# Local and global attention feeding a squared-ReLU MLP: heads loaded ahead of the transpose in SP's queue, value products on 128 columns of weights, and the second global pair's jobs a slot or two later

## The chip, the core and the metric

The kernel runs on one core of one Trainium2 chip. The metric is the device time of one execution in microseconds. Of the kernel before there are three timed runs, 1212.3, 1215.22 and 1217.07 us, median 1215.22 us. One more execution was profiled.

## The reference, cut to what matters

The input has 8 batches of 8 heads. Each head has 512 local positions and 32 global ones, all with 64 features. A local position attends to the local keys at most 32 positions away and to all 32 global keys; a global position attends to every key. The 64 features of the 8 heads are then put side by side, and a two-layer MLP with a squared ReLU follows.

```python
s_g = scale * np.matmul(q_g, k_all.transpose(0, 1, 3, 2))
out_g = np.matmul(sm(s_g), v_all)
...
s_l = np.concatenate([s_lg, s_ll], axis=-1)
a_l = sm(s_l)
out_l = np.matmul(a_l, np.concatenate([v_g, v_l], axis=2))
...
h = np.maximum(x @ w_in, 0.0)
return (h * h @ w_out).astype(np.float32)
```

## The kernel before, in words

**Work items.** A work item is one head of one batch on one half (256 queries) of the local positions. There are 128 such items, numbered `t`; the text calls them heads. Eight heads that share a batch and a half form a group of 256 tokens, which is one block of the MLP. The 16 groups give 16 blocks, and the global tokens of all batches (8 x 32) form a 17th. Each block takes 8 MLP steps, numbered `m`.

**The slot.** The main loop (L590) has one iteration per head, called a slot here. Slot `t` carries the attention of head `t`, the end of the attention of head `t - 1`, and MLP step `m = t - 9`. For the heads from 16 on ("not plain") the stations of a head are these:

- `load_head` (L91) loads queries and keys into `raw` (128 x 608 fp32), `load_v` (L103) loads the values into `v`. Both go through SP's queue. Both tiles have two buffers, so head `t + 2` can only be loaded into the buffer that head `t` has left.
- `split_qk` (L133) rounds `raw` to fp32r on ACT, and `split_qk_rest` (L143) makes the low parts on DVE. It runs in the slot before the one that uses it: slot `t` splits head `t + 1`.
- `scores` (L150, tile `s`) on PE, `softmax1` on DVE, `softmax2` (the exponentials) on ACT, `softmax3` (sums, reciprocal, scaling) on DVE; the result is `prob`, which has one buffer.
- `turn` (L218) splits the fp32 words of `prob` into two planes of 16 bits with three POOL copies into `planes`, and SP issues a DMA transpose of `planes` into `turned`. One slot later `join` (L226) puts the halves together again on POOL, into `joined`.
- `av` (L231) multiplies values and `joined` on PE in fp32, into the PSUM tile `xa`: three products of 256, 128 and 128 moving columns, each of them two instructions on PE. `x_evac` splits `xa` into `x_h` (ACT) and `x_l` (DVE), which the MLP reads nine slots later.

The plain heads (0 to 15) load query, key and value in one transfer and transpose on PE instead; their value products (tile names `pts` and `raw` in the rows) already take 128 columns of weights.

**PE in a slot.** `scores(t)` (rows `s`, four instructions), `gemm1` (rows `h`, 24), the global scores (rows `gs`, one), the first half of `gemm2` (rows `o`, six), `av(t - 1)` (rows `xa`, six), and the second half of `gemm2` (`o`, six). All but `xa` are fp32r.

**Global jobs.** Twice in 16 slots a set of four heads' global attention is carried through as a chain of jobs (L660 to L679), hung on slots relative to a slot `d`: maximum, exponential, `g_turn` and `g_join` (the same trip through POOL and the DMA transpose), `g_parts`, and for each of two pairs of heads a load of values, `g_split_v` (one ACT cast, two DVE subtractions), `g_av` (13 matmuls, rows `gxo`, and one ACT copy) and `g_x` (four DVE transposes). The number behind a job's slot is its place in the slot: 6 and 3 lie behind `turn`, 0 lies between `gemm1` and `gemm2`, 1 at the end of the slot. The two sets of 16 slots have `d` = 27 and 32, then 43 and 48, and so on, so that the tail of one lies beside the head of the next.

**What sets the order.** Every engine runs its instructions in the order of its queue. From slot 17 on, calls through the wrappers `pe`, `ve`, `ac`, `po`, `sp` are kept in the order in which the program makes them (L592); calls on `nc.sync` directly (`qr`, `gv`, the output) are put where the scheduler sees room. In slot `t` SP's calls were: `load_v(t)`, the transpose of `turn(t)`, `load_head(t + 2)`.

Of the kernel before, what the change touches and what calls it, by code (L numbers as in the profile page):

```python
# [7 lines left out]
F32 = mybir.dt.float32  # L8
# [9 lines left out]
P = 128  # L18
HALF = 256
NGR = 2 * B  # L20
NT = NGR * H
QC, KC, VC = HALF, 352, 256
QK, PK = QC + KC, QC + KC + VC
PS = QK + 192
WIN = 224
NEG = -1.6e10
NBLK = NGR + 1
# [2 lines left out]
NPLAIN = 16  # L30
# [8 lines left out]
def f(ap):  # L39
    return ap.bitcast(F32)  # L40
# [19 lines left out]
def attention_moe(  # L60
# [10 lines left out]
    pe, ve, ac, po, sp = (InOrder(tc, e) for e in (nc.tensor, nc.vector, nc.scalar, nc.gpsimd, nc.sync))  # L71
# [3 lines left out]
    p2 = ctx.enter_context(tc.tile_pool(name="p2", bufs=2))  # L75
# [3 lines left out]
    ps_a = ctx.enter_context(tc.tile_pool(name="ps_a", bufs=1, space=PSUM))  # L79

    heads = {}

    def plain(t):
        return t < NPLAIN
# [3 lines left out]
    def w_take(n):  # L88
        w_bufs["free"] -= n

    def load_head(t):  # L91
        if plain(t):
            w_take(1)
            raw = wp.tile([P, 1024], F32, tag="w", name=f"raw{t}")[:, :PK]
        else:
            raw = p2.tile([P, QK], F32, tag="raw", name=f"raw{t}")
        if t == 0:
            nc.sync.dma_start(raw[:, : QC + KC], pk[t, :, : QC + KC])
        else:
            sp.dma_start(raw, pk[t, :, : raw.shape[1]])  # L100
        heads[t] = dict(raw=raw)

    def load_v(t):  # L103
        v = heads[t]["v"] = p2.tile([P, 192], F32, tag="v", name=f"v{t}")
        sp.dma_start(v, pk[t, :, QK:PS])

    load_head(0)
    con = cp.tile([P, P + 4 * WIN], F32, name="con")
# [24 lines left out]
    def split_qk(t):  # L133

        if plain(t):
            return
        hd = heads[t]
        raw = hd["raw"]
        hi = hd["hi"] = p2.tile([P, QK + QC], F32R, tag="qk", name=f"qk{t}")
        hd["lo"] = hi[:, QK:]  # L140
        ac.copy(hi[:, :QK], raw[:, :QK])
# [66 lines left out]
    def transposes(t):  # L208
        pr = heads[t]["pr"]
        for i, (o, n) in enumerate(((0, 128), (320, 128), (128, 96), (224, 96))):  # L210
            pe.transpose(pt[:n, 128 * i : 128 * i + 128], pr[:, o : o + n], ident)

    def pt_copy(t):
        pts = p2.tile([P, 512], F32, tag="gh", name=f"pts{t}")
        ac.copy(pts, pt)
        heads[t]["pts"] = pts
# [9 lines left out]
    def join(t):  # L226
        joined = heads[t]["pts"] = p2.tile([P, 512], F32, tag="joined", name=f"joined{t}")
        words = joined.bitcast(U16).rearrange("p (n h) -> p h n", h=2)
        po.tensor_copy(words, turned.rearrange("p (h c) n -> p h (c n)", h=2))

    def av(t):  # L231
        hd = heads[t]
        c = QC + KC
        if plain(t):

            xa = ps_a.tile([P, HALF], F32, tag="xa", name=f"xa{t}")
            v, pts = hd["raw"][:, c:], hd["pts"]
            mm = [
                (xa, v[:, 0:128], pts[:, 256:512]),
                (xa[:, 0:128], v[:, 64:192], pts[:, 0:128]),  # L240
                (xa[:, 128:256], v[:, 128:256], pts[:, 128:256]),
            ]
        else:
            xa = ps_a.tile([64, HALF], F32, tag="xa", name=f"xa{t}")
            v, pts = hd["v"], hd["pts"]
            mm = [
                (xa, v[:, 128:], pts[:, 128:384]),
                (xa[:, 0:128], v[:, 0:64], pts[:, 0:128]),
                (xa[:, 128:256], v[:, 64:128], pts[:, 384:512]),
            ]  # L250
        for i, (o, a, b) in enumerate(mm):
            pe.matmul(o, a, b, start=i == 0, stop=i == len(mm) - 1, skip_group_check=True)
        hd["xa"] = xa[:64, :]
# [304 lines left out]
    def w_tick(t, place):  # L558
        if t < len(PLAN):
            for c in PLAN[t].split(",")[place]:  # L560
                {"b": w_pass, "s": w_chunk}[c]()

    def w_need(m):

        if m < 8:
            while w_next["bits"] < 8 * m + 8:
                n = w_next["bits"]
                w_pass()
                assert w_next["bits"] > n
        elif m < 16:  # L570
            while not set(range(4 * (m - 8), 4 * (m - 8) + 4)) <= whi.keys():
                n = w_next["split"]
                w_chunk()
                assert w_next["split"] > n, (m, w_next, w_bufs, sorted(w_used)[-1:])
# [15 lines left out]
    for t in range(NSTEP + LAG + 1):  # L590
        m = t - LAG
        ve.on, ac.on, pe.on, po.on, sp.on = [t >= x for x in FREE]  # L592
        prev, run = 1 <= t <= NT, 0 <= m < NSTEP
        live, early = t < NT, t < NPLAIN
        if t < NPLAIN - 8:
            load_head(t + 8)
        if run:
            w_need(m)
        old = prev and plain(t - 1)
        new = prev and not old  # L600
        if old:
            transposes(t - 1)
        if new:
            join(t - 1)
        if live and not early:
            load_v(t)
            scores(t)
        if old:
            pt_copy(t - 1)
        done = 0 < m <= NSTEP and m % 8 == 1 and m > 8  # L610
        if done:
            evac(m // 8 - 1)
        if live:
            softmax1(t)
        if run:
            gemm1(m, 0)
        if t + 1 < NT and not early and not done:
            split_qk(t + 1)
        if live:
            softmax2(t)  # L620
        if t + 1 < NT and not early and done:
            split_qk(t + 1)
        if live and not early:
            softmax3(t)
            turn(t)
        for job, *args in jobs.pop((t, 6), ()):
            job(*args)
        if NPLAIN <= t + 2 < NT:
            load_head(t + 2)
        for job, *args in jobs.pop((t, 3), ()):  # L630
            job(*args)
        w_tick(t, 0)
        if live and early:
            g_scores(t)
        if run:
            gemm1(m, 1)
        if old:
            av(t - 1)
        if live and not early:
            g_scores(t)  # L640
        if early and t + 1 < NPLAIN:
            scores(t + 1)
        if run:
            act1(m)
        if old:
            x_evac(t - 1)
            w_take(-1)
        if early:
            softmax3(t)
        w_tick(t, 1)  # L650
        if t + 1 == NPLAIN:
            split_qk(t + 1)
        if t + 1 < NT:
            split_qk_rest(t + 1)
        if live:
            if t % 2 == 1:
                g_evac(t)
            if t % 4 == 3 and t + 1 < NT:
                g_load(t + 1)
        if live and t % 4 == 3 and (t // 8) % 2 == 1:  # L660
            d = t if t % 8 == 3 else t + 1
            for at, *job in (
                (d + 1, 3, g_soft),
                (d + 1, 1, g_exp),
                (d + 2, 3, g_norm),
                (d + 2, 1, g_load_v, 0),
                (d + 3, 6, g_turn),
                (d + 4, 6, g_join),
                (d + 4, 3, g_split_v, 0),
                (d + 4, 1, g_load_v, 1),  # L670
                (d + 5, 3, g_parts),
                (d + 6, 0, g_av, 0),
                (d + 6, 1, g_split_v, 1),
                (d + 6, 1, g_x, 0),
                (d + 7, 0, g_av, 1),
                (d + 7, 1, g_x, 1),
            ):
                place, job, *args = job
                jobs.setdefault((at, place), []).append((job, t, *args))  # L679
        for job, *args in jobs.pop((t, 0), ()):  # L680
            job(*args)
        if m == NSTEP:
            for i in range(2):
                gemm2(m - 1, 0, (i,))
                gemm2(m - 1, 1, (i,))
                evac(NBLK - 1, (i,))
        elif m > 0:
            gemm2(m - 1, 0)
        if new:
            av(t - 1)  # L690
        if 0 < m < NSTEP:
            gemm2(m - 1, 1)
        if run:
            act2(m)
        if new:
            x_evac(t - 1)
        w_tick(t, 2)
        for job, *args in jobs.pop((t, 1), ()):
            job(*args)
        if 0 < m <= 8:  # L700
            w_done(m - 1)
        w_tick(t, 3)
        if 8 * NGR - 2 <= m < 8 * NGR:
            cols = (slice(0, 224), slice(224, HALF))[m % 2]
            ac.copy(x_h[:, 0, :, cols], xg[:, :, cols])
            ve.tensor_sub(x_l[:, 0, :, cols], xg[:, :, cols], f(x_h[:, 0, :, cols]))
# [75 lines left out]
```

## Time and profile before

The profiled execution took 1213.34 us on its own clock; its span from the first to the last instruction is 1211.6 us, so 1.7 us lie around it. It is 1.9 us under the median of the three timed runs.

| what | value |
|---|---|
| timed runs | 1212.3, 1215.22, 1217.07 us; median 1215.22 us |
| profiled execution, time / span | 1213.34 us / 1211.6 us |
| mean granted PE clock | 0.975 |
| DVE busy, share of the span | 645.9 us, 53% |
| ACT busy, share of the span | 618.3 us, 51% |
| POOL busy, share of the span | 400.4 us, 33% |

In the rows of the profile, PE is the matmul engine, PEld its weight loads, DVE the vector engine, ACT the scalar engine, POOL GpSimd and SPq the queue of SyncE, which issues the DMAs. A row of a timeline gives start and duration in us, then engine, line, operation, the tile written and the tiles read, and, in brackets, how long the engine had been idle and what ended that. L53 is the line of the wrapper, so the tiles tell the operations apart. A row of the chain of waits gives start, duration and the link.

### The profile page before, as it was taken

The page shows a single profiled execution, that of the slowest core. Times are in us where ns is not written, and L with a number is a line of the kernel's source. Part 1 is how long each engine was busy: PE and PEld are TensorE (multiplying, and loading weights), DVE is VectorE, ACT ScalarE, POOL GpSimd, SP SyncE. Part 2 cuts the span into 40 slices and gives each one's busy share as a digit, 9 for nine tenths or more (in the row PEclk, how much of TensorE's full clock was granted, in tenths as well). Part 3 has the DMA queues.
Part 4 walks back from the last instruction along what each step waited for, and adds up shares of the span by engine and source line. Part 5 has one row for each costly group of instructions (what it writes and reads, how often), then busy time and mean ns, then how long its engine had stood idle before and what let it go on. Part 6 is the DMA issues. An engine that isn't in the chain of part 4 may idle for free.

```text
span 1211.6 us, 19435 instructions
## 1 busy us (share of the span) xinstructions
PE 1101.4 (91%) x6704; PEld 913.3 (75%) x6704; DVE 645.9 (53%) x1997; ACT 618.3 (51%) x1519; POOL 400.4 (33%) x543
## 2 busy tenths in 40 slices
PE   8999899888998989979899889988999898999998
PEld 6776787777877768767776677777777676778987
DVE  5698655465554554555554755545454565544210
ACT  6897445464454545454544644545455454545332
POOL 1003433434334343334333443343433443433000
PEclk9999899999998999999999999999999999999999
DMA  9764434434444534345343434434434444343000
GB/s 369 276 222 91 94 93 103 91 102 91 96 105 102 109 90 109 77 99 126 81 106 81 108 93 101 94 91 111 91 81 109 91 116 97 93 90 71 23 18 18
DMA packets 209698, 127.63 MB, mean 105 GB/s; under 512 B 145344, under 2 KB 184768, under 8 KB 209600
## 3 DMA queue, kind: packets, MB, share of 16 engines
q1 hardware_dynamic: 209456, 126.33, 41.8%
q8 instruction: 53, 0.87, 0.3%
q14 instruction: 45, 0.37, 0.1%
q10 hardware_dynamic: 144, 0.07, 0.0%
HBM read 82.84 MB, written 8.91 MB: 76 GB/s over the span
## 4 chain that ended last, share of the span: by engine, by line
DMA 27%; PE 19%; ACT 16%; DVE 13%; POOL 10%; SPq 8%; issue 7%; POOLq 0%; DVEq 0%; ACTq 0%
DMA raw<-in_pk_dram 26%; POOL planes L53 8%; ACT prob L53 8%; SPq L53 8%; PE o L53 8%; PE h L53 7%; ACT qk L53 5%; DVE prob L53 3%; DVE st L53 3%; DVE qk L53 2%; PE xa L53 2%; POOL gp L53 2%; DMA turned<-planes 1%; PE s L53 1%; DVE gl L53 1%
## 5 line engine op out<-in xcount | busy, mean ns | idle before, releaser
L53 PE MATMUL h<-x_h,ws 128*128 128x256 f32 x2048 | 405.3, 291 | 0.0
L53 PEld LDWEIGHTS h<-x_h,ws 128*128 128x128 f32 x2048 | 341.9, 199 | 0.8
L53 PE MATMUL o<-ws,gh 128*128 128x512 f32 x1024 | 336.6, 410 | 0.0
L53 ACT CAST qk<-raw 128x608 fp32r<-128x608 f32 x112 | 78.3, 699 | 445.0 <-DMA raw<-in_pk_dram 444.9
L53 PE MATMUL h<-x_l,ws 128*128 128x256 f32 x1024 | 297.2, 290 | 0.0
L53 POOL COPY planes<-prob 128x448 uint16<-128x448 uint16 x336 | 190.3, 603 | 278.2 <-DVE prob L53 278.2
L53 POOL COPY joined<-turned 128x1024 uint16<-128x1024 uint16 x112 | 151.4, 1352 | 345.1 <-DMA turned<-planes 323.2
L53 DVE TENSOR_SCALAR st<-st 128x2 f32<-128x2 f32 x128 | 23.4, 183 | 381.4 <-ACT prob L53 377.4
L53 PEld LDWEIGHTS o<-ws,gh 128*128 128x128 f32 x1024 | 177.3, 190 | 43.7 <-issue 19.0
L53 PEld LDWEIGHTS h<-x_l,ws 128*128 128x128 f32 x1024 | 204.3, 200 | 1.0 <-DVE x_l L53 0.2
L53 PE MATMUL o<-ws,gl 128*128 128x512 f32 x512 | 203.4, 397 | 0.0
L53 PE MATMUL xa<-joined,v 128*64 128x128 f32 (+1 forms) x672 | 120.7, 316 | 37.5 <-POOL planes L53 24.3
L53 PEld LDWEIGHTS xa<-joined,v 128*64 128x64 f32 x672 | 76.5, 136 | 98.1 <-POOL planes L53 33.1
L53 PE MATMUL s<-qk 128*128 128x224 f32 x448 | 89.6, 306 | 61.5 <-DVE qk L53 56.5
L53 PEld LDWEIGHTS s<-qk 128*128 128x128 f32 x448 | 71.1, 200 | 96.5 <-ACT x_h L53 32.7
L53 DVE TENSOR_TENSOR qk<-raw,qk 64x352 fp32r<-64x352 f32 x224 | 132.4, 591 | 19.5 <-ACT qk L53 13.1
L53 DVE TENSOR_TENSOR gl<-pt,gh 128x512 fp32r<-128x512 f32 x128 | 87.2, 681 | 82.0 <-ACT gh L53 81.9
L53 PEld LDWEIGHTS o<-ws,gl 128*128 128x128 f32 x512 | 97.0, 189 | 22.9
L53 ACT ACTIVATE prob<-prob,st 128x224 f32<-128x224 f32 x224 | 105.8, 473 | 12.1 <-DVE st L53 12.1
L53 ACT ACTIVATE pt<-h 128x512 f32<-128x512 f32 x128 | 73.8, 577 | 66.3 <-PE h L53 66.1
L53 DVE CUSTOM_DVE_ANT_0 prob<-s,con 128x224 f32<-128x224 f32 x224 | 78.0, 385 | 24.0 <-PE s L53 21.4
L53 ACT ACTIVATE pt<-pt 128x512 f32<-128x512 f32 x128 | 74.5, 582 | 4.0
(74 smaller groups left out, 1182.2 us busy)
## 6 DMA issues: line engine op xcount, KB each, us to landing
raw<-in_pk_dram SPq DMA_DIRECT2D x113, 304.0 KB, 3.2
wr<-in_w_dram SPq DMA_DIRECT2D x32, 512.0 KB, 7.4
v<-in_pk_dram SPq DMA_DIRECT2D x112, 96.0 KB, 2.9
gv<-in_vg_dram SPq DMA_DIRECT2D x32, 320.0 KB, 3.8
out_dram<-ot SPq DMA_DIRECT2D x32, 256.0 KB, 3.6
raw<-in_pk_dram SPq DMA_DIRECT2D x15, 432.0 KB, 8.3
qr<-in_qg_dram SPq DMA_DIRECT2D x31, 64.0 KB, 2.8
turned<-planes SPq DMA_TRANSPOSE x112, 3.1
```

Source lines behind the costliest of these rows:

```text
L53: r = method(*args, **kwargs)
```

## The change

The changed kernel issues `load_head(t + 2)` at the start of slot `t`, ahead of `load_v(t)` and of `turn(t)`; before, it came behind `turn(t)`. `load_v` brings 256 instead of 192 columns, and the three value products take 128 columns of weights each, where they took 64, and write all 128 partitions of `xa`; the 64 extra rows of the result are not read. In the global jobs `g_split_v` of the second pair moves from slot `d + 6` to `d + 7` (and to place 3), `g_x` of the first pair from `d + 6` to `d + 8`, `g_av` of the second pair from `d + 7` to `d + 8` and its `g_x` from `d + 7` to `d + 9`; for the last set this last job stays in `d + 8`.

```diff
     def load_v(t):
-        v = heads[t]["v"] = p2.tile([P, 192], F32, tag="v", name=f"v{t}")
-        sp.dma_start(v, pk[t, :, QK:PS])
+        v = heads[t]["v"] = p2.tile([P, VC], F32, tag="v", name=f"v{t}")
+        sp.dma_start(v, pk[t, :, QK:PK])
...
-            xa = ps_a.tile([64, HALF], F32, tag="xa", name=f"xa{t}")
+            xa = ps_a.tile([P, HALF], F32, tag="xa", name=f"xa{t}")
             v, pts = hd["v"], hd["pts"]
             mm = [
                 (xa, v[:, 128:], pts[:, 128:384]),
-                (xa[:, 0:128], v[:, 0:64], pts[:, 0:128]),
-                (xa[:, 128:256], v[:, 64:128], pts[:, 384:512]),
+                (xa[:, 0:128], v[:, 0:128], pts[:, 0:128]),
+                (xa[:, 128:256], v[:, 64:192], pts[:, 384:512]),
             ]
...
         if new:
             join(t - 1)
+        if NPLAIN <= t + 2 < NT:
+            load_head(t + 2)
         if live and not early:
             load_v(t)
             scores(t)
...
-        if NPLAIN <= t + 2 < NT:
-            load_head(t + 2)
...
                 (d + 6, 0, g_av, 0),
-                (d + 6, 1, g_split_v, 1),
-                (d + 6, 1, g_x, 0),
-                (d + 7, 0, g_av, 1),
-                (d + 7, 1, g_x, 1),
+                (d + 7, 3, g_split_v, 1),
+                (d + 8, 3, g_x, 0),
+                (d + 8, 0, g_av, 1),
+                ((d + 8, 1, g_x, 1) if t == NT - 1 else (d + 9, 3, g_x, 1)),
```

The first place is SP's queue around slots 44 and 45. The number in a tile's name is the head (in `qr48` the head whose queries it serves), the rows `turned` are the transposes of `turn(44)` and `turn(45)` before, and of `turn(43)` and `turn(44)` in the changed kernel. Before:

```order
L53 DMA raw45_3471<-in_pk_dram 128x608
L285 DMA qr48_3842<-in_qg_dram 128x128
L53 DMA v44_3522<-in_pk_dram 128x192
L53 DMA_TRANSPOSE turned_95<-planes_94 128x8x128
L53 DMA raw46_3557<-in_pk_dram 128x608
L53 DMA v45_3605<-in_pk_dram 128x192
L53 DMA_TRANSPOSE turned_95<-planes_94 128x8x128
L53 DMA raw47_3640<-in_pk_dram 128x608
```

The same part of SP's queue in the changed kernel:

```order
L52 DMA raw45_3436<-in_pk_dram 128x608
L52 DMA v43_3438<-in_pk_dram 128x256
L52 DMA_TRANSPOSE turned_95<-planes_94 128x8x128
L52 DMA raw46_3522<-in_pk_dram 128x608
L284 DMA qr48_3842<-in_qg_dram 128x128
L52 DMA v44_3524<-in_pk_dram 128x256
L52 DMA_TRANSPOSE turned_95<-planes_94 128x8x128
L52 DMA raw47_3605<-in_pk_dram 128x608
```

The pattern of a transpose followed by a head and a value tile is the same, but the head that follows the transpose of `turn(t)` was `t + 2` and is now `t + 3`: every head stands one transpose earlier.

The second place is DVE's queue at the end of slot 33 and in slot 34, beside the global set of `d` = 27. The rows `ISA` are `softmax1`, the two rows `TENSOR_SCALAR` and `RECIPROCAL` on `st34` with the row on `prob` are `softmax3`, and `STREAM_TRANSPOSE` is `g_x`. Before:

```order
L53 TENSOR_TENSOR x_l_89<-xa32_2577,x_h_88 64x256
L53 TENSOR_TENSOR gvl27_1_2594<-gv27_1_2408,gvh27_1_2593 128x512
L53 TENSOR_TENSOR gvh27_1_2593<-gv27_1_2408,gvh27_1_2593 32x128
L53 STREAM_TRANSPOSE xg_90<-gxs27_0_2569 32x32 x4
L53 ISA prob_93,st34_2618<-s34_2607,con_78 128x224
L53 ISA st34_2618 128x1
L53 ISA prob_93,st34_2618<-s34_2607,con_78 128x224
L53 ISA st34_2618 128x1
L53 TENSOR_SCALAR st34_2618<-st34_2618 128x2
L53 RECIPROCAL st34_2618<-st34_2618 128x2
L53 TENSOR_SCALAR prob_93<-prob_93,st34_2618 128x224 x2
```

The same part of DVE's queue in the changed kernel:

```order
L52 TENSOR_TENSOR x_l_89<-xa32_2577,x_h_88 64x256
L52 ISA prob_93,st34_2611<-s34_2600,con_78 128x224
L52 ISA st34_2611 128x1
L52 ISA prob_93,st34_2611<-s34_2600,con_78 128x224
L52 ISA st34_2611 128x1
L52 TENSOR_SCALAR st34_2611<-st34_2611 128x2
L52 RECIPROCAL st34_2611<-st34_2611 128x2
L52 TENSOR_SCALAR prob_93<-prob_93,st34_2611 128x224 x2
L52 TENSOR_TENSOR gvl27_1_2640<-gv27_1_2408,gvh27_1_2639 128x512
L52 TENSOR_TENSOR gvh27_1_2639<-gv27_1_2408,gvh27_1_2639 32x128
```

The two subtractions of `g_split_v` move from ahead of the softmax of head 34 to behind it, and the four transposes leave this stretch; they now stand in slot 35. The first value product of the pair stays where it was on PE, and the second pair's 13 rows `gxo` move from slot 34 to slot 35. The order on POOL does not change.

More of the change, by code (lines that the diff above doesn't have):

```diff
@@ L23 @@
 QK, PK = QC + KC, QC + KC + VC
-PS = QK + 192
 WIN = 224
```

## The prediction

> **What bounds the kernel now.** I read the page first: busy shares, then the chain that ended last.
>
> ```profile
> PE 1101.4 (91%) x6704; PEld 913.3 (75%) x6704; DVE 645.9 (53%) x1997; ACT 618.3 (51%) x1519; POOL 400.4 (33%) x543
> ...
> DMA raw<-in_pk_dram 26%; POOL planes L53 8%; ACT prob L53 8%; SPq L53 8%; PE o L53 8%; PE h L53 7%; ACT qk L53 5%; DVE prob L53 3%; DVE st L53 3%; DVE qk L53 2%; PE xa L53 2%; POOL gp L53 2%; DMA turned<-planes 1%; PE s L53 1%; DVE gl L53 1%
> ```
>
> PE is busy 91%, so at first sight the matmuls bound it. But the chain passes through PE for 19% of the span only and through the landing of `raw` for 26%: some loop runs through that transfer. The chain in order of time shows it whole, here for one slot:
>
> ```profile
> 602.91 0.70 ACT qk L53
> 603.61 0.95 ACT prob L53 x4
> ...
> 604.99 0.35 DVE prob L53
> ...
> 607.16 1.23 SPq L53
> ...
> 608.45 3.30 DMA raw<-in_pk_dram
> 611.77 0.70 ACT qk L53
> ```
>
> ACT casts one head (602.91), does the exponentials of the head before it, DVE scales, POOL copies the planes, SP issues their transpose (1.23 us), and only behind it in SP's queue the next `raw` (608.45), which lands 3.3 us later; then ACT casts again, 8.86 us after the first cast. ACT runs in order, so everything behind the cast waits too. The row of the list of waits, and two casts from ACT's timeline, give the pace:
>
> ```profile
> ACT qk L53 <- DMA raw<-in_pk_dram: 444.9, 103, 7.2
> ```
>
> ```profile
> 103.79 0.70 ACT L53 CAST qk<-raw 128x608 fp32r<-128x608 f32 x1 [0.84 <-DMA raw<-in_pk_dram]
> ...
> 1090.09 0.70 ACT L53 CAST qk<-raw 128x608 fp32r<-128x608 f32 x1 [4.52 <-DMA raw<-in_pk_dram]
> ```
>
> ACT waits for `raw` 103 times, 444.9 us. The casts are those of heads 18 and 127, the third and the last of 112. From the one to the other are 109 slots and 986.3 us: **9.05 us a slot**, which is the loop's length, longer where a global transpose stands in SP's queue too. Of PE alone a slot needs less. Three stretches, from the table of windows (length, then PE busy, PEld, DVE, ACT, POOL, granted clock, DMA):
>
> ```profile
> 981.24:989.51 8.27, 8.27 (x62) 7.13 (x61) 5.98 (x24) 4.65 (x12) 2.94 (x5) 1.00 0.68 194
> 1061.17:1068.61 7.44, 7.44 (x50) 6.32 (x48) 4.14 (x14) 4.28 (x12) 3.03 (x4) 1.00 0.23 63
> 1130.00:1209.00 79.00, 76.29 (x490) 68.11 (x488) 13.62 (x27) 27.69 (x49) 0.00 (x0) 1.00 0.05 16
> ```
>
> The second is a slot without any PE idle: 7.44 us. The first is one with the 13 `gxo` matmuls, 8.27 us, so these cost 0.83 us. In both DVE, ACT and POOL are busy for 6 us or less. The third, the MLP alone at the end, has PE busy 76.3 of 79 us, and its clock is 1.00. So PE idles some 1.4 us a slot for a loop that PE isn't in.
>
> **The change: loading ahead.** The transfers and their order in the queue keep their pattern, but the head behind a given transpose is one further on. It is issued at the same moment and needed a slot later: 3.3 us of landing against more than 7. The wait of 444.9 us goes. What `load_head(t + 2)` itself waits for is the last read of `raw` of head `t`, by DVE in slot `t - 1`:
>
> ```profile
> 606.82 0.70 PE L53 MATMUL s<-qk 128*128 128x224 f32 x4
> ...
> 607.16 1.23 SPq L53 DMA_TRANSPOSE turned<-planes  x1
> ...
> 607.96 0.39 DVE L53 CUSTOM_DVE_ANT_0 prob<-s,con 128x224 f32<-128x224 f32 x1
> ...
> 608.45 0.57 SPq L53 DMA_DIRECT2D raw<-in_pk_dram  x1
> ...
> 609.12 0.39 SPq L53 DMA_DIRECT2D v<-in_pk_dram  x1
> ...
> 610.34 1.35 POOL L53 COPY joined<-turned 128x1024 uint16<-128x1024 uint16 x1 [3.20 <-DMA turned<-planes]
> ...
> 614.32 1.68 POOL L53 COPY planes<-prob 128x448 uint16<-128x448 uint16 x3 [2.63 <-DVE prob L53]
> 614.46 1.27 DVE L53 TENSOR_TENSOR qk<-raw,qk 64x352 fp32r<-64x352 f32 x2
> ```
>
> That read (614.46, two subtractions) starts with the plane copies (614.32) and ends before them, so before the transpose ahead of the load: no new wait. Behind the load in SP's queue stand `v` and the next transpose; both are needed much later. `v` grows from 96 to 128 KB; 304 KB of `raw` land in 3.3 us (608.45) and 96 KB of `v` in 2.9, and `v` is needed a slot later: nothing.
>
> ```profile
> v<-in_pk_dram SPq DMA_DIRECT2D x112, 96.0 KB, 2.9
> ```
>
> What is late next? Three paths, by the rows above. (1) Scores to scores: `s` starts at 606.82, `softmax1` at 607.96 (1.14 us on), its two halves take 0.9, exponentials to scaled `prob` 2.0 (603.61 to 605.6), the subtractions 1.27: 5.3 us, then the next `s` may run. (2) The transpose: 3.18 us from issue (607.16) to `join` (610.34), 1.35 for `join`, 1.68 for the planes: 6.2 us. (3) ACT and DVE by sum: 6 us at most in the windows. All are under 7.1, so **PE becomes the bound**.
>
> **The change: 128 columns.** Around `xa`, first as it is (64 columns), then in an early head with 128 columns:
>
> ```profile
> 1064.05 0.29 PE L53 MATMUL gs<-qk,qgz 128*128 128x288 f32 x1
> 1064.18 0.62 PE L53 MATMUL o<-ws,gh 128*128 128x512 f32 x2
> 1064.64 0.40 PE L53 MATMUL o<-ws,gl 128*128 128x512 f32 x1
> 1064.87 0.63 PE L53 MATMUL o<-ws,gh 128*128 128x512 f32 x2
> 1065.34 0.39 PE L53 MATMUL o<-ws,gl 128*128 128x512 f32 x1
> 1065.66 1.08 PE L53 MATMUL xa<-joined,v 128*64 128x256 f32 x6
> 1066.67 0.73 PE L53 MATMUL o<-ws,gh 128*128 128x512 f32 x2
> 1067.24 0.40 PE L53 MATMUL o<-ws,gl 128*128 128x512 f32 x1
> ```
>
> ```profile
> 99.59 1.04 PE L53 MATMUL xa<-pts,raw 128*128 128x256 f32 x6
> 100.39 0.38 PE L53 MATMUL gs<-qk,qgz 128*128 128x288 f32 x1
> 100.60 1.02 PE L53 MATMUL o<-wf,r 128*128 128x512 f32 x2
> ```
>
> An `o` matmul normally follows the last after 0.23 us (1064.18, 1064.64, 1064.87: three in 0.69). Before `xa` it takes 0.32 (0.09 more); the six `xa` take 1.01; the two `o` behind take 0.57 where two take 0.46 (0.11 more). With 128 columns six `xa` and one `gs` take 1.01 (99.59 to 100.60); a `gs` alone takes 0.13 (1064.05 to 1064.18), so the six take 0.88, 0.13 less. Together 0.33 us a head. The early group goes from fp32 to fp32r and back to fp32 without a gap, so what costs is the switch to 64 columns, not the type. On 112 heads that is 37 us of PE, worth nothing while the loop binds and all of it once PE does. The lower bound is no gain at all.
>
> The load itself is dearer:
>
> ```profile
> L53 PEld LDWEIGHTS xa<-joined,v 128*64 128x64 f32 x672 | 76.5, 136 | 98.1 <-POOL planes L53 33.1 <-issue 30.6 <-POOL joined L53 16.8
> ...
> L53 PEld LDWEIGHTS xa<-pts,raw 128*128 128x128 f32 x96 | 15.0, 190 | 4.6 <-ACT pts L53 3.3
> ```
>
> 136 ns become 190, 54 more on six loads a head, 0.32 us. In the early group four `xa` steps fit into what is left of 0.88 us, about 0.11 each, so the loads hide under the matmuls; I cost them at nothing, the upper bound is 112 x 0.32 = 36 us. The Trainium skill (TensorE: Matmul & The Clock Gate, "LDWEIGHTS (loading the stationary operand)") has a load take its number of columns divided by 1.2 in ns, so twice as long for 128 columns, and would speak against the change; the difference it gives, 53 ns, agrees with the 54 here, and paid in full it would take back the 36 us.
>
> **The change: jobs.** Nothing is added, so the sum on each engine stays. DVE's pieces by the groups of instructions:
>
> ```profile
> L53 DVE STREAM_TRANSPOSE xg<-gxs 32x32 f32<-32x32 f32 x128 | 25.7, 201 | 2.0
> ...
> L53 DVE TENSOR_TENSOR gvl<-gv,gvh 128x512 fp32r<-128x512 f32 x32 | 21.9, 686 | 2.3 <-ACT gvh L53 2.3
> ...
> L53 DVE TENSOR_TENSOR gvh<-gv,gvh 32x128 fp32r<-32x128 f32 x32 | 12.4, 387 | 0.7
> ```
>
> `g_split_v` (0.69 + 0.39) and `g_x` (4 x 0.20) leave the end of a slot, where they held up the next softmax, for the place ahead of the subtractions, on path (1). That path has 7.1 - 5.3 = 1.8 us to spare. The heaviest slot, `d + 4` of the second set, now gets both, 1.88 us: just over. The second set's `g_turn` overwrites what the moved `gxo` read, so POOL now waits there for PE; but these matmuls end under 4.6 us after the scores start (0.7 for the scores, 2.88 from the first `h` at 1061.17 to `gs` at 1064.05, 0.13, 0.83), and POOL's plane copies, queued before, end only after 5.3 by path (1), whose subtractions they accompany. In the last set the global values come a slot later, just before the last block: under 1 us.
>
> **The sum**, against the profiled execution, 1213.3 us (span 1211.6 plus 1.7 around it, 1.9 under the median shown). 109 slots at 7.44 - 0.33 = 7.11 us are 775; 28 `gxo` groups at 0.83 add 23; 798 against 986.3 now. For what still waits I take 15 us: about 1 us in each of the seven rounds of 16 slots for the overfull slot and its neighbours, and 8 for slots 17 to 22, where ACT and DVE also split weights. That is an estimate, between 0 and the rival below. 986 - 813 = 173 saved; the ends give and take under 1. **1213 - 173 = 1040; 1041 us.** With no wait left it is 1024 at least. These 7.11 us have the clock at 1.00, as the windows have it; at the mean of 0.975 that the profile gives for the whole span the 813 us would be some 20 more, inside the forecast's own range.
>
> **The rivals.** *The transpose binds next.* Path (2) has only 0.9 us of slack. One `raw` landing in the same chain took 4.28 us instead of 3.3:
>
> ```profile
> 617.36 4.28 DMA raw<-in_pk_dram
> ```
>
> A transpose slowed likewise gives 7.3 us a slot (0.2 x 109 = 22 us) and, in 14 slots with a global trip through POOL (1.8 us more), about 1 us each: some 40 us on the forecast, 1065 to 1095, say 1081. For it: it is the longest path left; against it: nothing in the row of transposes stands behind anything new. *The wide weights bring nothing*: the 0.33 us stay, 1041 + 37 = 1078, and if the dearer loads show, 1114. Against it: the early heads. *The change doesn't load ahead*: if SP's queue reaches the load no earlier, because the buffer is released later than I read it, the loop stays at 9.05, PE's gain hides in it, and the time stays at 1208 to 1217. *Slower*: the load now stands ahead of the transpose. If the buffer of head `t` comes free only when the planes of slot `t` are ready, the issues of `raw` and `v` (0.57 and 0.39 us at 608.45 and 609.12) delay each transpose by 0.96 us in a loop that then is 10.0: 109 x 0.96 = 105, 1318 us. It decides when DVE's subtractions end a slot later than they do now; they end with the copies of the slot before, about 7 us ahead of that point.
>
> **How the numbers follow.** Forecast, PE-bound, 1024 to 1065: 0.66. Transpose: 0.14. Wide weights without gain: 0.06, half of it under 1095. Something between 1095 and 1205 that I don't see: 0.05. No loading ahead: 0.05. Slower: 0.04. The range 1024 to 1095 holds 0.83. Within 0.5% (6 us, about what a measurement can tell from no change) is 0.05, slower 0.04, faster 0.91.
>
> **What would show it.** ACT's wait for `raw` gone from the list of waits; casts 7.3 us apart on average; PE busy near 100% between 100 and 920 us with a clock of 1.00; `xa` six in 0.88 us and `o` at 0.23 on both sides; the chain on PE rather than DMA. Wrong if POOL's or PE's wait for `joined` grows, if DVE's subtractions hold `s`, or if `h` and `o` step slower than now.

## The result, and the profile after

The changed kernel takes **1043.63 us** (median of four runs, 1042.34 to 1047.13) against 1215.7 us (1212.3 to 1217.07, four runs) of the kernel before: a ratio of 0.8593, interval 0.8565 to 0.8621, 172 us less. The prediction was 1041 us, in 1024 to 1095. The profiled execution took 1042.34 us with a span of 1040.6 us.

From the page of the changed kernel, the span, the busy times, the granted clock in 40 slices, and the chain that ended last, by engine:

```profile
span 1040.6 us, 19456 instructions
...
PE 1021.9 (98%) x6704; PEld 912.6 (88%) x6704; DVE 696.7 (67%) x1997; ACT 634.2 (61%) x1519; POOL 396.3 (38%) x543
...
PEclk9999999999999999999999999999999999999999
...
PE 89%; ACT 4%; DVE 4%; DMA 1%; issue 1%; DVEq 0%; ACTq 0%; SPq 0%
```

PE is busy 98% instead of 91%, but the row that tells more is the last: the chain lies on PE for 89% of the span, before for 19%, and on DMA for 1%. The matmuls do not only fill the time now, they set it. Rows of the list of waits (engine and tile, what it waited for, us in total, times, longest):

```profile
POOL joined L52 <- DMA turned<-planes: 309.0, 102, 5.6
...
POOL gp L52 <- PE gxo L52: 19.6, 4, 19.0
ACT qk L52 <- DMA raw<-in_pk_dram: 14.1, 4, 5.9
```

ACT waited for `raw` 103 times, 444.9 us; now 4 times, 14.1 us. The largest wait left, POOL's for the transpose, is not in the chain that ended last: POOL is early. The pace, from the casts of the same two heads (18 and 127) in ACT's timeline:

```profile
103.03 0.70 ACT L52 CAST qk<-raw 128x608 fp32r<-128x608 f32 x1 [0.78 <-DMA raw<-in_pk_dram]
...
916.02 0.70 ACT L52 CAST qk<-raw 128x608 fp32r<-128x608 f32 x1
```

813.0 us for 109 slots, **7.46 us a slot** on the mean instead of 9.05. From the table of windows (columns as in the prediction; a slot runs from its first `h` matmul to that of the next) a plain slot, slot 68 (an overfull one), slots 17 to 22 together, and all slots after them:

```profile
430.87:437.99 7.12, 7.12 (x49) 6.52 (x48) 4.55 (x14) 4.41 (x11) 2.60 (x5) 1.00 0.49 117
...
489.85:497.36 7.51, 7.49 (x50) 6.53 (x48) 6.20 (x17) 4.48 (x10) 4.54 (x6) 1.00 0.62 140
```

```profile
103.10:157.50 54.40, 48.23 (x317) 40.27 (x316) 41.13 (x102) 31.98 (x76) 22.33 (x31) 1.00 0.47 108
157.50:923.90 766.40, 765.37 (x5215) 698.66 (x5215) 549.25 (x1596) 473.85 (x1155) 353.45 (x480) 1.00 0.52 124
```

In the plain slot PE has no idle time. In the 766 us of the last row it idles 1.0 us; in the 54 us before, the slots in which the weights of the MLP are still being split, it idles 6.2. The chain in order of time through one slot of the changed kernel, which in the kernel before went through ACT, DVE, POOL, SP and the landing of `raw`:

```profile
430.59 0.44 PE s L52 x4
431.03 2.88 PE h L52 x24
433.91 0.13 PE gs L52
434.04 1.40 PE o L52 x6
435.44 0.88 PE xa L52 x6
436.31 1.40 PE o L52 x6
437.71 0.44 PE s L52 x4
```

### The profile page after: what moved, and what is told of

It is laid out like the page before. It is cut to its first block, busy times and chain, and to the rows that moved or that the text cites. A ratio compares the mean times of both kernels' runs of the same rounds, so it can differ in the third digit from the quotient of the medians.

```text
span 1040.6 us, 19456 instructions
## 1 busy us (share of the span) xinstructions
PE 1021.9 (98%) x6704; PEld 912.6 (88%) x6704; DVE 696.7 (67%) x1997; ACT 634.2 (61%) x1519; POOL 396.3 (38%) x543
## 4 chain that ended last, share of the span: by engine, by line
PE 89%; ACT 4%; DVE 4%; DMA 1%; issue 1%; DVEq 0%; ACTq 0%; SPq 0%
PE h L52 35%; PE o L52 34%; PE xa L52 10%; PE s L52 6%; PE gxo L52 2%; PE gs L52 2%; DMA raw<-in_pk_dram 1%; ACT pr L52 1%; ACT wf L52 1%; ACT ws L52 1%; DVE qk L52 1%; DVE st L52 1%; ACT prob L52 1%; DVE ws L52 0%; PE pt L52 0%
## 5 line engine op out<-in xcount | busy, mean ns | idle before, releaser
L52 PE MATMUL h<-x_h,ws 128*128 128x256 f32 x2048 | 389.2, 283 | 0.2 <-ACT x_h L52 0.2
L52 PE MATMUL o<-ws,gh 128*128 128x512 f32 x1024 | 332.4, 406 | 0.0
L52 PEld LDWEIGHTS h<-x_h,ws 128*128 128x128 f32 x2048 | 327.5, 191 | 1.3 <-ACT x_h L52 0.6
L52 PE MATMUL h<-x_l,ws 128*128 128x256 f32 x1024 | 289.4, 283 | 0.0
L52 POOL COPY planes<-prob 128x448 uint16<-128x448 uint16 x336 | 179.8, 572 | 114.9 <-DVE prob L52 114.9
L52 PEld LDWEIGHTS h<-x_l,ws 128*128 128x128 f32 x1024 | 196.2, 192 | 0.9
L52 PEld LDWEIGHTS xa<-joined,v 128*128 128x128 f32 x672 | 107.9, 190 | 24.4 <-issue 3.9
L52 PE MATMUL xa<-joined,v 128*128 128x128 f32 (+1 forms) x672 | 117.3, 310 | 3.9 <-POOL planes L52 2.3
L52 DVE TENSOR_SCALAR st<-st 128x2 f32<-128x2 f32 x128 | 52.5, 411 | 96.9 <-ACT prob L52 92.9
L52 ACT CAST qk<-raw 128x608 fp32r<-128x608 f32 x112 | 78.1, 698 | 15.2 <-DMA raw<-in_pk_dram 14.1
L52 ACT CAST x_h<-xa 64x256 fp32r<-64x256 f32 x120 | 44.0, 366 | 55.6 <-PE xa L52 53.4
```

The source lines that it names most:

```text
L52: r = method(*args, **kwargs)
```

## The experiments

The theory (T): before, the loop through the landing of `raw` sets the pace; loading ahead opens it; PE then sets the pace, so that only then a shorter `xa` counts; the moved jobs are worth next to nothing. Rivals: the 128 columns or the job moves open the loop by themselves; the wider load gives back what the columns save; the transpose or ACT binds next. The kernels e1 to e4, e5 to e8 and e9 to e12 each ran on one chip with the kernel before beside them (medians 1219.0, 1221.2 and 1215.0 us). "Loop" is the time from the cast of head 18 to that of head 127 in the profiled execution.

| kernel | median us | ratio to before, interval | loop us |
|---|---|---|---|
| e1: load ahead alone | 1075.21 | 0.8815 (0.8786 to 0.8844) | 843.95 |
| e2: 128 columns alone | 1218.98 | 0.9999 (0.9977 to 1.002) | 989.63 |
| e3: job moves alone | 1217.35 | 0.999 (0.9965 to 1.0014) | 985.29 |
| e4: changed, load late again | 1223.01 | 1.0029 (1.0007 to 1.0051) | 994.80 |
| e5: changed, 64 columns again | 1074.47 | 0.8801 (0.8785 to 0.8818) | 843.40 |
| e6: changed, jobs at old places | 1038.69 | 0.8506 (0.849 to 0.8523) | 809.22 |
| e7: changed, 96 columns | 1044.23 | 0.8548 (0.8528 to 0.8569) | 814.45 |
| e8: changed, fewer weights in slots 19 to 22 | 1040.93 | 0.8525 (0.8509 to 0.8542) | 810.76 |
| e9: before, second cast | 1284.98 | 1.0562 (1.0516 to 1.0608) | 1054.60 |
| e10: changed, second cast | 1047.22 | 0.861 (0.8583 to 0.8636) | 814.91 |
| e11: changed kernel again | 1044.58 | 0.8588 (0.8562 to 0.8615) | 815.39 |
| e12: three edits on top | 1036.04 | 0.852 (0.8494 to 0.8547) | 806.48 |

**One part alone, and all but the load (e1 to e4).** e1 is the kernel before with this edit only; e2 and e3 have only the hunks on `v`, `xa` and its three products, and only the job lines, of the change shown above; e4 is the changed kernel with e1's edit taken back.

```diff
+        if NPLAIN <= t + 2 < NT:
+            load_head(t + 2)
         if live and not early:
             load_v(t)
...
             turn(t)
         for job, *args in jobs.pop((t, 6), ()):
             job(*args)
-        if NPLAIN <= t + 2 < NT:
-            load_head(t + 2)
```

> Only load_head moves; value products stay on 64 columns and the jobs where they were. Theory (the loop through raw sets the pace, then PE binds): PE slots of 7.44 us instead of 7.11, so the changed kernel's 1044 plus 109 x 0.33 = 36, 1080 us, and up to 15 more if the jobs at their old places hold up a softmax: 1078 to 1095. Rival (the jobs' places bind as soon as the load is ahead): above 1100. Rival (the parts add up in proportion): about 1080 too, told apart by the next kernel.

> Only the 128 columns. Theory: the loop through raw still sets 9.05 us a slot and PE's 0.33 us go into its idle time: 1208 to 1217 us, no change. Rival (PE is the bound all along and each part saves its own share): 1216 - 37 = 1179.

> Only the jobs move. Theory: the loop stays; where g_split_v and g_x stood on it at a slot's end (1.9 us, 14 times) they leave it for a place beside it, at most 14 x 1.9 = 27 us gained: 1190 to 1217. Rival (the jobs are what made the slots long): below 1180.

> The changed kernel with load_head behind turn again. Theory: the loop is back, ACT waits for raw about 100 times again, time as with the other two parts alone: 1190 to 1217. Rival (each part saves its share): about 1044 + 135 = 1179.

The row of ACT's wait for `raw` in the lists of waits of e1, e2, e3 and e4, each from its own trace:

```profile
ACT qk L53 <- DMA raw<-in_pk_dram: 10.8, 4, 4.1
```

```profile
ACT qk L53 <- DMA raw<-in_pk_dram: 446.9, 103, 7.4
```

```profile
ACT qk L53 <- DMA raw<-in_pk_dram: 406.1, 106, 6.9
```

```profile
ACT qk L52 <- DMA raw<-in_pk_dram: 420.5, 102, 7.0
```

Only the place of the load decides whether ACT waits: gone in e1, there in all others. e1 alone gives 144 us, and came out 3 us under its range. e2 gives nothing (its time is that of the kernel before on this chip, which lies 2 us over the range), though its PE work is shorter (busy 1087.5 us against 1101.4): PE waits that much longer. e3 takes 39 us of waiting away from that row, yet the loop is 1 us from that of before; the waiting only stands elsewhere. Its 1217.35 us lie 0.35 over its range; the kernel before took 1219.0 on this chip. e4 was expected at 1217 at most and is 4 us slower than before, with a ratio just above 1 (lower end 1.0007); why its loop is 5 to 10 us longer than those of e2 and e3 stays open. Two scores in PE's timeline of e1, one slot apart:

```profile
434.60 0.60 PE L53 MATMUL s<-qk 128*128 128x224 f32 x4
...
442.03 0.60 PE L53 MATMUL s<-qk 128*128 128x224 f32 x4
```

7.43 us: PE's own slot with 64 columns (7.44 in the prediction). So with the load ahead PE binds at once, and the next step is PE's.

**The columns under a bound PE (e5, e7).** e5 puts the 64 columns back, with `v` still 256 wide; e7 takes 96.

```diff
-            xa = ps_a.tile([P, HALF], F32, tag="xa", name=f"xa{t}")
+            xa = ps_a.tile([64, HALF], F32, tag="xa", name=f"xa{t}")
...
-                (xa, v[:, 128:], pts[:, 128:384]),
-                (xa[:, 0:128], v[:, 0:128], pts[:, 0:128]),
-                (xa[:, 128:256], v[:, 64:192], pts[:, 384:512]),
+                (xa, v[:, 128:192], pts[:, 128:384]),
+                (xa[:, 0:128], v[:, 0:64], pts[:, 0:128]),
+                (xa[:, 128:256], v[:, 64:128], pts[:, 384:512]),
```

```diff
-            xa = ps_a.tile([P, HALF], F32, tag="xa", name=f"xa{t}")
+            xa = ps_a.tile([96, HALF], F32, tag="xa", name=f"xa{t}")
...
-                (xa, v[:, 128:], pts[:, 128:384]),
-                (xa[:, 0:128], v[:, 0:128], pts[:, 0:128]),
-                (xa[:, 128:256], v[:, 64:192], pts[:, 384:512]),
+                (xa, v[:, 128:224], pts[:, 128:384]),
+                (xa[:, 0:128], v[:, 0:96], pts[:, 0:128]),
+                (xa[:, 128:256], v[:, 64:160], pts[:, 384:512]),
```

> The changed kernel with 64 columns of weights again (v stays 256 wide). Theory: two gaps around xa and slower xa steps, 0.33 us on each of 112 slots that PE bounds: 1044 + 37 = 1081 (1077 to 1085). Rival (the dearer load of 128 columns takes back what the gaps cost, or the gaps came from late joins): 1040 to 1050.

> The changed kernel with 96 columns of weights and 96 rows of xa. If the gaps come from switching PE between a part of 64 columns and the whole, 96 columns count as the whole and it stays at 1042 to 1046. If any change in the number of columns costs them: 1077 to 1085.

e5, 3 us under its range, is 30 us slower than e7 on the same chip: the columns are worth 30 us once PE binds, and nothing before (e2). e5 also has the moved jobs and e1 has not, and both take 64 columns: 1074.47 and 1075.21 us, with ratios whose intervals overlap. So with 64 columns the moves are neither a gain nor a loss that these runs can tell (e5's `v` is wider too). Now `xa` in the changed kernel's PE timeline (the fourth column is what the line does, the last the number of instructions):

```profile
434.58 0.63 PE L52 MATMUL o<-ws,gh 128*128 128x512 f32 x2
435.05 0.39 PE L52 MATMUL o<-ws,gl 128*128 128x512 f32 x1
435.27 1.04 PE L52 MATMUL xa<-joined,v 128*128 128x256 f32 x6
436.07 0.71 PE L52 MATMUL o<-ws,gh 128*128 128x512 f32 x2
436.62 0.39 PE L52 MATMUL o<-ws,gl 128*128 128x512 f32 x1
```

The `o` ahead of `xa` steps by 0.22 (435.05 to 435.27), the six `xa` take 0.80, the two `o` behind 0.55; 1.57 us for what took 1.90 before (0.32, 1.01, 0.57), 0.33 less. The predicted 0.88 for the six and 0.46 for the two `o` behind are 0.80 and 0.55 here, with the same sum: the cost only shows a little later. The rows of the early head in the prediction had it so already (99.59 to 100.39, and 0.21 instead of 0.13 for the `gs` behind). Weight loads, by shape, of e5 (64 columns), e7 (96) and the changed kernel (128): count, then busy us and mean ns:

```profile
L52 PEld LDWEIGHTS xa<-joined,v 128*64 128x64 f32 x672 | 76.5, 136 | 63.3 <-POOL planes L52 25.8 <-issue 17.7 <-POOL joined L52 2.0
```

```profile
L52 PEld LDWEIGHTS xa<-joined,v 128*96 128x96 f32 x672 | 95.9, 163 | 33.7 <-POOL planes L52 5.5 <-issue 3.5 <-POOL joined L52 1.4
```

```profile
L52 PEld LDWEIGHTS xa<-joined,v 128*128 128x128 f32 x672 | 107.9, 190 | 24.4 <-issue 3.9
```

A load takes 27 ns more for each 32 columns, and the time doesn't follow it: 96 and 128 columns come out alike (1044.23 us; 1043.63 and 1044.58 on other chips), 64 columns with the cheapest load are the slow ones. So the load is hidden. The difference for which the prediction cites the Trainium skill (TensorE: Matmul & The Clock Gate, "LDWEIGHTS (loading the stationary operand)"), by its rule an estimate of 53 ns from 64 to 128 columns, is there in the rows (54) and isn't paid. The times themselves are not as the rule gives them, 53 and 107 ns: the rows have 136 and 190, and the rows decide.

Where the 0.33 us lie is in the steps from one start to the next, here as medians over the 112 groups in the traces of e5 (64 columns) and of the changed kernel (128), in ns. The last `o` ahead takes 320 and 229, the first `xa` 267 and 215, the next four 216, 109, 109, 109 and 215, 108, 112, 112, the last `xa` 203 and 31, the first `o` behind 336 and 316. With 96 columns (e7) they are those of 128 within 3 ns. So it is not that each product with 64 columns is slower: the cost stands at the two edges of the group, where PE goes over to 64 columns and back.

But 64 columns alone are not enough for it. The 13 `gxo` of the same kernel have 64 columns as well, between `gs` and `o` with 128, and they are fp32r like these neighbours. From PE's timeline, slot 67:

```profile
484.44 0.30 PE L52 MATMUL gs<-qk,qgz 128*128 128x288 f32 x1
484.57 0.22 PE L52 MATMUL gxo<-gvh,pth 128*64 128x128 f32 x1
...
485.29 0.22 PE L52 MATMUL gxo<-gvh,pth 128*64 128x128 f32 x1
485.35 0.67 PE L52 MATMUL o<-ws,gh 128*128 128x512 f32 x2
485.85 0.40 PE L52 MATMUL o<-ws,gl 128*128 128x512 f32 x1
```

`gs` takes 0.13 before `gxo` as it does before `o`, the last `gxo` takes 0.06 as the others do, and only the two `o` behind take 0.50 instead of 0.46: some 0.05 us for both edges. So what costs 0.33 us here is 64 columns in these fp32 products, among fp32r products of 128. `gxo` differs from `xa` in the type and in the length of its moving operand, and which of them makes the difference no run shows: no kernel took `xa` in fp32r. The Trainium skill (TensorEngine Tiling (Array Packing), "Key Properties") says that changing the tiling mode drains TensorE, and its list has configurations with 64 columns and none with 96; whether a plain matmul with 64 columns is such a mode it doesn't say, and it gives no price. The edges of `xa` look like it, those of `gxo` don't, so that rule is not borne out as the cause.

**The jobs and slots 17 to 22 (e6, e8).** e6 puts the job lines back as they were before the change. e8 splits six more weight tiles in slots 17 and 18, so that fewer are left from 19 on (two entries of the list that sets the splits of each slot).

```diff
-                (d + 7, 3, g_split_v, 1),
-                (d + 8, 3, g_x, 0),
-                (d + 8, 0, g_av, 1),
-                ((d + 8, 1, g_x, 1) if t == NT - 1 else (d + 9, 3, g_x, 1)),
+                (d + 6, 1, g_split_v, 1),
+                (d + 6, 1, g_x, 0),
+                (d + 7, 0, g_av, 1),
+                (d + 7, 1, g_x, 1),
```

```diff
-PLAN = [..., "ss,s,s,s", "ss,s,s,s", "s,,s,", "s,,s,", "s,,s,", "s,,s,", "s,,s,", "s,,s,"]
+PLAN = [..., "ss,s,s,s", "ss,s,s,s", "ss,s,s,s", "ss,s,s,s", "s,,s,", "s,,s,", "s,,s,", "s,,s,"]
```

> The changed kernel with the jobs at their old places. Theory: g_split_v and g_x at a slot's end push the next softmax1 back by 1.9 us less what the slot has to spare; path 1 has 1.8 us: 1042 to 1060. Rival (the job moves carry a large part): above 1065.

> The changed kernel with the last seven weight splits in slots 17 and 18 instead of spread to slot 20. The last raw weight tile shares the two buffers of raw, so slots 18 to 20 load heads late, about 8 us in all. Theory: the buffer comes free two slots sooner and 2 to 6 us go: 1038 to 1042. Rival: two slots overfull on DVE and ACT cost as much again: 1043 to 1048.

e6 missed its range on the low side: without the job moves the kernel is **faster**, by 5.5 us against e7 on the same chip (profiled executions: span 1037.4 against 1042.5). With the wide weights that part of the change costs time. A small reason stands in the rounds of 16 slots. All engines of the changed kernel in slot 68, which is slot `d + 4` of a second set and is 0.38 us longer than a plain one:

```profile
492.58 0.84 DVE L52 STREAM_TRANSPOSE xg<-gxs 32x32 f32<-32x32 f32 x4
...
493.69 2.10 POOL L52 COPY sg<-gq 128x1280 uint16<-128x1280 uint16 x1
...
494.30 1.56 DVE L52 TENSOR_TENSOR gvh<-gv,gvh 32x128 fp32r<-32x128 f32 x1
...
495.89 0.98 DVE L52 TENSOR_TENSOR qk<-raw,qk 64x352 fp32r<-64x352 f32 x2
...
496.92 0.41 PEld L52 LDWEIGHTS s<-qk 128*128 128x128 f32 x3 [0.21 <-DVE qk L52]
```

The first row is the moved `g_x` of the first set. It pushes this set's own `g_split_v` under POOL's copy `sg`, and there its small subtraction `gvh` took 1.56 us, where the group took 0.28 to 0.54 before. The subtractions on `qk` behind it end late, and the scores wait for them (the bracket). The same place in DVE's queue in e6, with no `g_x` ahead:

```profile
492.62 0.55 DVE L52 TENSOR_TENSOR gvh<-gv,gvh 32x128 fp32r<-32x128 f32 x1
493.20 1.09 DVE L52 TENSOR_TENSOR qk<-raw,qk 64x352 fp32r<-64x352 f32 x2
```

There it takes 0.55, `sg` starts only at 493.96, and slot 68 takes 7.13 us instead of 7.50. The larger reason stands in slots 18 to 20. The chain of the changed kernel in order of time there:

```profile
115.42 1.80 DVE gvl L52
...
117.23 0.55 DVE gvh L52
...
119.65 0.42 DVE qk L52
...
120.30 3.42 DMA raw<-in_pk_dram
...
123.75 0.70 ACT qk L52
124.45 0.95 ACT prob L52 x4
...
129.39 0.44 DVE qk L52
...
129.89 2.93 DMA raw<-in_pk_dram
...
138.17 1.55 DVE gvh L52
...
140.47 3.21 DMA raw<-in_pk_dram
```

Here alone, but for the first load of the kernel, the landing of `raw` is in the chain still. The last raw weight tile uses one of `raw`'s two buffers until it is split in slot 20, so the load of a head waits for DVE's last read of the head before it (129.83), and the loop is closed again: landing, cast, exponentials, DVE, landing. The moved `g_split_v` (`gvl` and `gvh`, 2.35 us from 115.42) stands on DVE ahead of the read that releases the buffer, so inside this loop; at its old place, the end of the slot before, it stood behind the read of that slot. The moved `g_x` stands in it too (four transposes each from 126.41 and from 136.53, 0.75 us each time), and the `gvh` of 1.55 us is the small subtraction of the next set's own `g_split_v`, again beside `sg`.

How much each reason is worth can be read from the slots. Of the 5.2 us between the loops of e7 and e6, 4.4 lie in slots 17 to 22 (56.2 and 51.8 us) and 0.9 in all slots from 23 on (766.05 and 765.17), where the old places have a long slot of their own (slot 34 takes 8.61 us instead of 7.95). e8 gains 3.3 us against e7, all of it in slots 17 to 22 (52.0), and ACT's wait for `raw` falls from 14.1 us to 3.9. These six slots are also what differs between executions of one order: 54.4 us in the changed kernel and 56.4 when it was run again (e11), while the slots from 23 on take 766.3 and 766.7.

**Is ACT's cast in the loop, and out of it now? (e9, e10).** The cast of 0.70 us is made twice, in the kernel before and in the changed one.

```diff
         ac.copy(hi[:, :QK], raw[:, :QK])
+        ac.copy(hi[:, :QK], raw[:, :QK])
```

> The kernel before with split_qk's cast done twice (0.70 us of ACT more in each of 112 slots). Theory: the cast is a link of the loop, which gets 0.70 us longer: 109 x 0.70 = 76, about 1295 us (1275 to 1300). Rival (PE sets the pace and ACT, busy 51%, has room): no change, 1215 to 1225.

> The changed kernel with the same second cast. Theory: PE sets the pace, ACT's sum of some 4.4 us in a slot of 7.1 has room, and the cast has a slot to spare: 1042 to 1050. Rival (the loop is only shorter and still binds, or ACT binds next): 76 us more, about 1120.

The kernel before gets 70 us longer, in the loop 0.63 us for each of 109 slots, close to the whole cast, although ACT was busy only 51% of it. The changed kernel gets 2.6 us longer than e11 on the same chip, though ACT is busier there (711.4 us of 1043.7); its loop in the profiled execution is no longer than that of e11 (814.9 and 815.4 us). This is the plainest sign that the cast lay on what set the pace and no longer does: a second one cost nine tenths of its length, and is now nearly free. That the landing of `raw` lay there as well is shown by e1 and e4.

**The changed kernel again, and a better version (e11, e12).** e12 has e6's and e8's edits, and makes the calls of the jobs at place 0 ahead of `g_evac`, so that ACT's copy `gxs`, which empties the PSUM tile that `xa` takes next, comes first in ACT's queue. In an odd slot it stands behind the copies of `g_evac`, and `xa` waits for it: slot `d + 3` of the second set takes 8.30 us instead of 7.97 in the changed kernel, slot `d + 7` with the jobs at their old places (e6).

```diff
+        for job, *args in jobs.pop((t, 0), ()):
+            job(*args)
         if live:
             if t % 2 == 1:
                 g_evac(t)
...
-        for job, *args in jobs.pop((t, 0), ()):
-            job(*args)
```

> The changed kernel once more, on the chip of the next: 1042 to 1049.

> The changed kernel with the jobs at their old places, the copy gxs ahead of the copies of the global scores on ACT, and the last weight splits in slots 17 and 18. If the three gains add up: 5 from the jobs' places, 3 from the splits, 7 x 0.3 = 2 from gxs, 10 us under the changed kernel: 1033 to 1037. If the splits and the old places get in each other's way in slots 17 to 20: 1038 to 1042.

1036.04 us, 8.5 us (0.8%) under e11 on the same chip, with ranges that don't touch (1035.05 to 1037.38, 1043.33 to 1045.3). From slot 24 on every slot but one (8.62 us) is 7.11 to 7.13 us, or 7.93 to 7.95 with a `gxo` group, which is PE's own length. In the profiled executions, 5.2 us of the gain against e11 lie in the slots from 23 on (761.5 us) and 3.6 in slots 17 to 22. Those take 52.8 us, no less than with either edit alone (51.8 in e6, 52.0 in e8): there the two gains did not add up.

## Why the prediction was right

- **What bounded the kernel before** was read rightly. The chain named the landing of `raw`, at 91% busy PE. e9 shows it from the other side: lengthening the loop lengthens the kernel, shortening PE (e2) doesn't. The 9.05 us are a mean, though, and not the length of one loop: of the 109 slots 31 took PE's own length already (7.43 to 7.46 us, 8.27 or 8.28 with `gxo`), others up to 13.6.
- **Loading ahead removes the wait**: 444.9 to 14.1 us, and e1 and e4 show that it alone does. The load's buffer was free in time, as worked out, except in slots 18 to 20. There the last raw weight tile has the other buffer, which the prediction did not look at, and what the rival called *Slower* describes did happen for a few us: the planes were ready at 127.5, but their transpose was issued at 130.96, behind the `raw` that waited until 129.89.
- **PE becomes the bound**: 7.12 us a plain slot with no PE idle, 7.11 predicted; path (2), the transpose, did not bind. The mean clock is 0.999 instead of 0.975 in the profiled executions (0.996 in the other three of the changed kernel). That ACT and DVE need 6 us at most by sum did not quite hold: DVE is busy 6.20 of slot 68's 7.51 us.
- **128 columns**: 0.33 us a head, as predicted, and the dearer load is hidden. The reason given, the switch to 64 columns "and not the type", is right about the edges but goes too far: `gxo` makes the same switch in fp32r for some 0.05 us. On the whole kernel e5 shows 30 us rather than 37: slots that wait for something else anyway (17 to 22, 55.4 us in e5 and 56.2 in e7, and the overfull ones) don't gain, which the sum of 112 heads left out.
- **15 us of waits** in the sum of 813 us. The measured loop is 813.0. Counted from the slots, slots 17 to 22 have about 9 (54.45 us, less six times 7.11 and three `gxo` groups at 0.83), and the six rounds behind them about 0.7 each (0.33 in slot `d + 3`, 0.38 in `d + 4` of the second set), 5 in all with slot 24. The place was right; the estimate of 1 us a round was a little high. That the sum met the loop to a few tenths is luck: slots 17 to 22 alone took 2 us more when the same kernel ran again (e11).
- **The jobs** were the mis-sized term. They were costed by their DVE time alone, 1.88 us against 1.8 free, hence about 0.1 us a round; taking the moves back gave 5.5 us (e6 against e7). With them moved, the overfull slot lost 0.38 us, because the small subtraction lengthened from 0.39 to 0.71 us on the mean, and in slots 18 to 20 the moved work stands in a loop that the prediction took for open. By the slots the second is the larger part. That `gp` would have to wait for `gxo` at no cost held (19.6 us in four waits, none in the chain).
- **The ends**: the loop saved 173.3 us, the execution 171.0. From the last cast to the end it takes 124.6 us instead of 121.5, and about as long in e1 and e6 (125.4, 124.3), so the moved jobs are not the cause. With the cast no longer late, it stands further ahead of PE: the last head's scores start 8.0 us behind its cast, before 3.6. Counted from these scores the end is 116.5 us, before 117.8, so the end itself lost nothing.

## What to carry to other kernels

Where an engine is busy 90% and the chain of waits runs mostly elsewhere, look for the loop that closes over a queue: here one load behind one transpose made 9.05 us a slot on the mean, against 7.74 with that load ahead and nothing else changed (e1), and lengthening a step of the loop on purpose (e9) shows with one edit whether the step lies on it. An edit that shortens an engine's work can be worth nothing until that engine binds (e2, e5), so try such edits again after each change of the bound. And once an engine binds, work that was moved to spare it should be tried at its old place again: here one of three edits in a change that gained 172 us was a loss of some 5 beside the wide weights (e6, e7), and neither gain nor loss without them (e1, e5).

## What the runs showed of the hardware that was not expected

- Six fp32 matmuls with 64 columns of weights between fp32r matmuls with 128 cost 0.33 us more than with 128, all of it at the two edges of the group; with 96 columns there is no such cost, and 13 fp32r matmuls with 64 columns between such neighbours cost some 0.05 us.
- DVE's 1997 instructions, the same in number, took 696.7 us instead of 645.9, and in e1, where the jobs are not moved, 685.6. Not all of them got longer: 29 us of the 51 are one group of 128 rows, `TENSOR_SCALAR` on `st`, whose mean went from 183 to 411 ns. In 48 of these rows DVE started while POOL's copy `joined` ran, and each ended 21 to 27 ns behind the end of that copy; the 68 rows with no POOL work beside them took 0.17 us. The kernel before had 3 such long rows. One of the 48:

```profile
482.98 1.35 POOL L52 COPY joined<-turned 128x1024 uint16<-128x1024 uint16 x1 [3.31 <-DMA turned<-planes]
...
483.37 0.98 DVE L52 TENSOR_SCALAR st<-st 128x2 f32<-128x2 f32 x1 [0.80 <-ACT prob L52]
```

- The subtraction on 32 x 128 elements (`gvh`) does the same beside POOL's copy `sg`: 7 of its 32 rows took 1.55 to 1.57 us, all beside that copy and all ending 80 to 89 ns behind its end, and the other 25, none of them beside it, 0.55 or less. Its mean is 708 ns, against 387 before. All these rows end as if DVE waited for the POOL copy of 16-bit words to be done. That the copy is the cause is read from these ends; no run moved it by itself:

```profile
L52 DVE TENSOR_TENSOR gvh<-gv,gvh 32x128 fp32r<-32x128 f32 x32 | 22.6, 708 | 0.5
```
